# Weight chunks spread differently over the slots, and the mean of the first token group behind the scores: thresholded attention followed by a feed-forward block

## The chip, the cores and the metric

The kernel runs on one core of one Trainium2 chip. The metric is the time of one execution in device microseconds (us), the median of several runs. The engines are named as in the profile: PE (TensorE, with its weight loads as PEld), DVE (VectorE), ACT (ScalarE), POOL (GpSimd) and SP (SyncE, which here issues nearly all DMAs). Each engine works through its own instructions in the order in which the program wrote them; semaphores order the engines among each other.

## The reference

Inputs are q, k, v of 8 batches, 8 heads, 576 tokens and 64 features in float32, a scalar tau, a gain g_ln of 512, and two weights, 512 x 2048 and 2048 x 512. The weights come as float64: the kernel gets their raw 64-bit words and makes float32 of them itself.

```python
scores = scale * np.matmul(q, k.transpose(0, 1, 3, 2))
thresh = np.max(scores, axis=-1, keepdims=True) - tau
scores = np.where(scores >= thresh, scores, -1000000000.0)
scores = scores - np.max(scores, axis=-1, keepdims=True)
attn = np.exp(scores)
attn = attn / (np.sum(attn, axis=-1, keepdims=True) + 1e-09)
attn_out = np.matmul(attn, v)
# (B,H,S,D) -> x of (B, S, H*D)
mu = np.mean(x, axis=-1, keepdims=True)
var = np.mean((x - mu) ** 2, axis=-1, keepdims=True)
xn = (x - mu) / np.sqrt(var + 1e-06) * g_ln
ch = np.maximum(xn @ w_ch1, 0.0) @ w_ch2
out = x + ch
```

## The kernel before

**Slots.** The attention is cut into 72 slots, nine for each batch (`SLOTS`), handled by the loop `for n in range(NS)`. A slot takes 128 rows of each of four score blocks: two heads (h = 0 and 1, one PSUM region `sc` each) by two blocks of queries. The first four slots of a batch take the first 256 queries of a head pair, the fifth (s equal to `HP`, which is 4) takes the last 64 queries of all heads, and the last four take the second 256. In one slot these steps follow each other, and they are spread over this slot and the next two:

- `turn` (L345) transposes the q and k of the pair needed in the next slot, on DVE, after POOL has scaled q (L356). `load_qk` fetches them through SP.
- `scores` (L391, L408) writes the two `sc` regions on PE.
- `exponentials` (L414): DVE takes the negated row maxima (`neg`, L422), POOL makes the thresholds from them (`thr`, L426), ACT makes the exponentials (L436).
- `weights` (L438): DVE masks the exponentials by the threshold and sums them (L443). It reads `sc`, so the scores of the next slot cannot be written before it. In batch 0 ACT then makes diagonal matrices of the reciprocal sums (L457).
- In batch 0 `turn_weights` (L473) transposes and scales the weights on PE (`tp` and `tr`), with ACT copying out (L493, L516); later batches transpose on DVE (L533), store to a DRAM scratch (L538) and load it again (L547, L552).
- `values_of` (L565, L591, L601) multiplies with v on PE; ACT copies the result into the token group's `x` (L609, L614), and POOL adds up the features in `sum` (L643).

**Groups.** A batch holds two token groups of 288 tokens. When a group is complete, `group_ready` arranges its `mean_of` (a PE product with a matrix of 1/512, L652), `centre` (DVE subtracts the mean, L666) and `ffn_steps`, the feed-forward part as a queue of PE products (L101: `p` and `seg`). `second_part` feeds products from this queue between the attention steps, four times a slot. Group 0 is ready in slot 6 (`ready(0)` is 24 quarters). PE's order is thus fixed when the program is built.

**Weights.** The 32 weight chunks of 512 KB (16 of w1, then 16 of w2) go through the class `Weights`:

- `fetch(most)` issues up to that many loads on SP (L252), as far as there are free rooms; the rooms are places in tiles that are not needed yet.
- `begin_to(count)` begins chunks until so many have been begun: two DVE instructions (L271, L275) and two on ACT (L279, L283) each.
- `carry_all` adds the low words on POOL (L289) and frees the raw room; `mask_all` finishes a chunk on DVE (L298); `scale_all` multiplies a w1 chunk by g_ln on POOL (L310).

The table `BEGUN` gives, for each slot, the count of chunks begun by three places in the slot: after the scores' second half has been prepared, behind the masking, and at the slot's end. The feed-forward products need w1 in the order of the chunks, and then w2.

**Warm products.** `constants(times)` issues that many PE products of constants whose result is not read; there are 22 ahead of slot 0 and 8 ahead of the scores of slots 2, 3 and 4.

Of the kernel before, what the change touches and what calls it, by code (L numbers as in the profile page):

```python
# [18 lines left out]
def kernel(  # L19
# [36 lines left out]
    HP = H // 2  # L56
# [39 lines left out]
    def product(out, lhsT, rhs, **flags):  # L96


        for h in range(2):
            r = slice(64 * h, 64 * h + 64)  # L100
            nc.tensor.matmul(out[r], lhsT=lhsT[:, r], rhs=rhs, **flags)  # L101
# [239 lines left out]
    def by_blocks(u):  # L341

        return units[u][0] > 0
# [47 lines left out]
    def scores(b, s):  # L391


        hp, half = (s, 0) if s < HP else (s - HP - 1, 1)

        pieces = []
        for h in range(2):
            t = 0
            for j in range(2):
                first = FREE + j * S  # L400
                for at, n in span(first, S):
                    pieces.append((t, h, j, at, n, at - first))
                    t += n
        for t, h, j, at, n, o in sorted(pieces):
            r = slice(64 * h, 64 * h + 64)
            for i in range(2):
                qT, kT, ql = turned[b * HP + (2 * j + i if s == HP else hp)]
                nc.tensor.matmul(  # L408
                    sc[h][64 * i : 64 * i + 64, at : at + n],
                    lhsT=ql[r] if s == HP else qT[r, half, j * 128 + 64 * i : j * 128 + 64 * i + 64],  # L410
                    rhs=kT[r, o : o + n], start=True, stop=True,
                )

    def exponentials(n):  # L414


        neg = small.tile([128, 4], F32, tag="neg", name="neg")
        thr = small.tile([128, 4], F32, tag="thr", name="thr")
        es = e_room[(n + 1) % 2 if n < SLOTS else 0]
        for h in range(2):  # L420
            i = slice(2 * h, 2 * h + 2)
            nc.vector.tensor_reduce(  # L422
                out=neg[:, i], in_=pairs[h],
                axis=AXL.X, op=ALU.max, negate=True,
            )
            nc.gpsimd.tensor_scalar(  # L426
                out=thr[:, i], in0=neg[:, i], scalar1=-1.0, scalar2=low_sb,
                op0=ALU.mult, op1=ALU.add,
            )
            if h == 0:  # L430
                conversion.scale_all()
        run(n, "copy")
        for i in range(4):
            if i == 2:
                yield es, thr
            nc.scalar.activation(es[:, i], blocks[i], func=AF.Exp, bias=neg[:, i : i + 1])  # L436
# [254 lines left out]
    def run_first(calls):  # L691
        for fn in calls[:1]:
            calls.pop(0)
            fn()

    def run_all(calls):
        now = calls[:]
        calls.clear()
        for fn in now:
            fn()  # L700
# [236 lines left out]
    def ffn_steps(g):  # L937
        rb = yield from first_part(g)
        yield from (second_quarters if g else second_plain)(g, rb)
# [3 lines left out]
    QUARTERS = 4  # L943
# [10 lines left out]
    def at_quarter(n, i, fn, *args):  # L954
        later_calls.setdefault((n, i), []).append((fn, args))

    def run(n, i):
        for fn, args in later_calls.pop((n, i), ()):
            fn(*args)

    def ready(g):

        if g < 2:
            return (24, 42)[g]
        b, t = divmod(g, 2)
        return QUARTERS * (b * SLOTS + (HP, 2 * HP)[t] + 2) + (2, 4)[t]

    def second_part(n, i):

        nonlocal issued, owed, part, now  # L970
        part, now = i, QUARTERS * n + i
        if not queue:
            return
        at = QUARTERS * n + i
        g = sum(issued >= e for e in ends)
        left = sum(ROOM[t % QUARTERS] for t in range(at, ready(g + 1))) if g + 1 < NG else 0
        owed += (ends[g] - issued) * ROOM[i] / left if left > 0 else 8


        got = 1 if i in (0, QUARTERS - 1) else 2  # L980
        while queue and (owed >= 0.5 or got == 1 and i in (0, QUARTERS - 1)):
            got, cost = next(queue[0], (None, 0))
            if got is None:
                queue.pop(0)
                got = 1
            elif got == 0:
                owed = 0.0
                break
            else:
                issued += cost  # L990
                owed -= cost

    def group_ready(g):
        first = divmod(ready(g), QUARTERS)
        before = divmod(ready(g) - 1, QUARTERS)
        at_quarter(*before, mean_of, g)
        at_quarter(*(first if g and first[1] else before), centre, g)
        at_quarter(*first, lambda: queue.append(ffn_steps(g)))

    conversion = Weights()  # L1000
    if w_ch1.dtype == I64:
        conversion.fetch(4)
    else:
# [10 lines left out]
        conversion.scaled = conversion.n1  # L1014

    BEGUN = [
        (0, 0, 2), (3, 3, 4), (6, 6, 7), (9, 9, 10), (12, 12, 13), (15, 15, 16),
        (18, 20, 21), (23, 25, 26), (28, 30, 31), (32, 32, 32),
    ]

    def constants(times):

        warm = ps_ff.tile([128, QH], F32, tag="ff", name="warm")
        for _ in range(times):
            product(warm[:, :128], lhsT=avg_sb, rhs=ident, start=True, stop=True)
# [4 lines left out]
    for n in range(NS):  # L1030
        b, s = divmod(n, SLOTS)
        masks_at, behind_at, end_at = BEGUN[min(n, len(BEGUN) - 1)]
        run(n, -3)
        if 1 < n <= HP:
            constants(8)
        scores(b, s)
        run(n, -2)
        run(n, -1)
        rest = exponentials(n)
        es, thr = next(rest)  # L1040
        run(n, 0)
        if n >= HP:
            conversion.fetch(2)
        run_first(stores)
        second_part(n, 0)
        while drops and drops[0][0] is nc.gpsimd:
            drops.pop(0)[-1]()
        next(rest, None)

        u = (n + 1) // SLOTS * HP + (n + 1) % SLOTS  # L1050
        if (n + 1) % SLOTS < HP and u < len(units):
            turn(u)
            if u + 1 < len(units):
                load_qk(u + 1)
        if n < HP:
            conversion.fetch(2)
        if n < SLOTS + HP:
            run_all(aside)
        conversion.mask_all()
        conversion.begin_to(masks_at)  # L1060
        conversion.carry_all()
        conversion.scale_all()
        run(n, 1)
        second_part(n, 1)
        blocks_go = by_blocks(b * HP)
        diags = weights(es, thr, blocks_go)
        run_all(aside)
        drip()
        if n < SLOTS:
            run_all(stores)  # L1070
        conversion.mask_all()
        conversion.begin_to(behind_at)
        run(n, 2)
        second_part(n, 2)
        conversion.carry_all()
        box = []
        if blocks_go:
            scr = turn_blocks(s, es)
            at_quarter(n + 1, 0, lambda s=s, scr=scr, box=box: box.append(fetch(s, scr)))
        else:  # L1080

            made = turn_weights(s, es, diags)
            for i, at in enumerate(
                (-1, -1, 0, 0) if s <= HP else (-1, -1, -1, -1) if s < 2 * HP else (-1, 0, 1, 2)
            ):
                if i < 3:
                    at_quarter(n + 1, at, next, made)
                else:
                    at_quarter(n + 1, at, lambda made=made, box=box: box.append(next(made)))
        at_quarter(  # L1090
            n + 1, 1 if b == 0 and s <= HP else 3,
            lambda b=b, s=s, box=box: values_of(b, s, box[0]),
        )
        if s in (HP, 2 * HP):
            group_ready(2 * b + (s > HP))
        run_all(aside)
        drip({nc.vector: 4, nc.gpsimd: 6})
        conversion.fetch(2)
        if n >= HP + 2:
            conversion.mask_all()  # L1100
        run(n, 3)
        if b == 0 and s < HP - 2:
            load_v(s + 2)
        elif n >= SLOTS - 2 and (n + 2) % SLOTS < HP and n < NS - 2:
            load_v((n + 2) // SLOTS * HP + (n + 2) % SLOTS)
        second_part(n, 3)
        conversion.begin_to(end_at)
        conversion.carry_all()
        run_all(aside)
        drip({nc.vector: 2, nc.gpsimd: 0})  # L1110
# [40 lines left out]
```

## Time and profile before

| what | value |
|---|---|
| median of 3 runs | 1389.49 us (1386.02 to 1389.49) |
| profiled execution | 1386.68 us |
| its span, first to last instruction | 1384.9 us, mean granted clock 0.991 |
| busy: PE | 1329.0 us (96%), 17544 instructions |
| busy: PEld | 1002.4 us (72%) |
| busy: DVE | 922.7 us (67%) |
| busy: ACT | 455.3 us (33%) |
| busy: POOL | 617.9 us (45%) |
| DMA | 206.88 MB, mean 149 GB/s |

A busy share is an average over the whole span; the change concerns the first sixth of it, so the profile is read there, slot by slot. In the trace before, the scores of slots 0 to 6 start at 10.06, 18.42, 32.63, 46.86, 60.51, 71.80 and 88.84 us, those of slots 7 to 10 at 117.92, 141.09, 163.80 and 187.88 us. In lines of a timeline the columns are start and duration in us, engine, line, operation, what is written and read, and the count; in brackets stands the idle time before it and what ended it. In lines on waits the numbers are the sum in us, how often, and the longest. "SPq" is SP's queue issuing a DMA.

### The profile page before, as it was taken

The numbers are of one execution on the slowest core, as the hardware profiler recorded it, in microseconds if no ns is written. First come the engines' busy times: TensorE is split into PE (matmuls) and PEld (weight loads), VectorE is DVE, ScalarE is ACT, GpSimd is POOL, SyncE is SP. The second block draws the span as 40 slices with busy tenths as digits, with TensorE's granted clock in tenths as the row PEclk, the third lists the DMA queues.
The fourth block names the chain that finished last, engine by engine and source line by source line (L and its number), as shares of the span: only waits on it lengthen the run. The fifth ranks groups of instructions, "written<-read, shape, count | busy, mean of one in ns | idle before, by whom it ended". The sixth has DMA issues, their size and how long they took to land.

```text
span 1384.9 us, 40781 instructions
## 1 busy us (share of the span) xinstructions
PE 1329.0 (96%) x17544; PEld 1002.4 (72%) x17544; DVE 922.7 (67%) x1638; ACT 455.3 (33%) x991; POOL 617.9 (45%) x823
## 2 busy tenths in 40 slices
PE   6878989999999999999999999999999999999996
PEld 5755655867768696877869687776868677686966
DVE  6987867676776767657776667657776767766211
ACT  4766523232332323232232323323232323323120
POOL 3554344544443544443444455353444445344313
PEclk9999999999999999999999999999999999999998
DMA  9912255447734576447754476345763476443211
GB/s 207 267 49 70 66 145 156 160 145 184 203 131 164 139 197 178 145 143 187 200 158 147 152 198 183 135 164 154 190 187 132 144 186 186 135 160 134 58 17 18
DMA packets 322020, 206.88 MB, mean 149 GB/s; under 512 B 247984, under 2 KB 279472, under 8 KB 313776
## 3 DMA queue, kind: packets, MB, share of 16 engines
q1 hardware_dynamic: 317072, 203.68, 50.8%
q8 instruction: 138, 2.26, 0.7%
q10 hardware_dynamic: 4736, 0.59, 0.4%
q14 instruction: 42, 0.34, 0.1%
q0 software_dynamic: 32, 0.00, 0.0%
HBM read 120.46 MB, written 83.76 MB: 147 GB/s over the span
## 4 chain that ended last, share of the span: by engine, by line
PE 86%; DVE 5%; issue 2%; DMA 2%; POOL 2%; ACT 2%; SPq 1%; POOLq 0%; DVEq 0%; ACTq 0%
PE p L101 37%; PE seg L101 27%; PE sc L408 9%; PE sc L591 8%; PE sc L601 2%; DVE neg L422 1%; DMA v_rest<-in_v_dram 1%; PE tp L101 1%; DVE e L443 1%; PE mean L101 1%; PE var L101 0%; POOL sum L643 0%; POOL q_in L356 0%; SPq L136 0%; ACT e L436 0%
## 5 line engine op out<-in xcount | busy, mean ns | idle before, releaser
L101 PE MATMUL p<-xc,w 128*64 128x288 f32 x4096 | 518.1, 408 | 14.6 <-ACT hidden L795 5.0
L101 PEld LDWEIGHTS p<-xc,w 128*64 128x64 f32 x4096 | 288.2, 137 | 222.3 <-issue 15.8
L422 DVE TENSOR_REDUCE neg<-sc 128x2 f32<-128x1152 f32 x144 | 188.7, 1351 | 241.7 <-PE sc L408 241.2
L101 PE MATMUL seg<-hidden,w 128*64 128x144 f32 x3840 | 248.3, 287 | 3.8 <-DVE hidden L865 3.8
L101 PEld LDWEIGHTS seg<-hidden,w 128*64 128x64 f32 x3840 | 234.8, 137 | 15.6 <-issue 7.5
L459 POOL TENSOR_SCALAR e<-e,den 128x576 f32<-128x576 f32 x252 | 194.0, 782 | 114.9 <-DVE den L448 114.9
L443 DVE SCALAR_TENSOR_TENSOR e<-sc,thr,e 128x576 f32<-128x576 f32 x288 | 221.9, 809 | 19.8 <-POOL thr L426 14.4
L426 POOL TENSOR_SCALAR thr<-neg,low_sb 128x2 f32<-128x2 f32 x144 | 42.4, 295 | 424.3 <-DVE neg L422 422.2
L795 ACT ACTIVATE hidden<-p 128x288 f32<-128x288 f32 x256 | 106.4, 416 | 324.1 <-PE p L101 324.0
L436 ACT ACTIVATE e<-sc,neg 128x576 f32<-128x576 f32 x288 | 197.6, 754 | 4.8 <-DVE neg L422 4.8
L533 DVE STREAM_TRANSPOSE et<-e 128x1152 f32<-128x1152 f32 x112 | 153.1, 1373 | 18.3 <-POOL e L459 17.5
L408 PE MATMUL sc<-kT,qT 64*64 64x384 f32 (+3 forms) x2048 | 144.5, 413 | 11.2 <-DVE e L443 10.4
L591 PE MATMUL sc<-em,v_in 128*64 128x128 f32 (+1 forms) x2368 | 129.5, 263 | 0.0
L591 PEld LDWEIGHTS sc<-em,v_in 128*64 128x64 f32 x2368 | 122.9, 137 | 7.8
L101 PE MATMUL seg<-hidden,stage 128*64 128x144 f32 x1920 | 123.3, 286 | 0.0
L101 PEld LDWEIGHTS seg<-hidden,stage 128*64 128x64 f32 x1920 | 117.6, 137 | 2.9 <-issue 2.9
L408 PEld LDWEIGHTS sc<-kT,qT 64*64 64x64 f32 x2048 | 78.0, 136 | 56.2 <-issue 24.1
L614 ACT COPY x<-sc 128x128 f32<-128x128 f32 x120 | 31.7, 266 | 247.7 <-PE sc L408 181.2
L865 POOL TENSOR_TENSOR hidden<-hidden 128x576 f32<-128x576 f32 x60 | 84.8, 1427 | 47.5 <-ACT hidden L795 37.9
L880 ACT COPY part<-seg 128x288 f32<-128x288 f32 x75 | 30.2, 403 | 198.4 <-PE seg L101 194.3
L865 DVE TENSOR_TENSOR hidden<-hidden 128x576 f32<-128x576 f32 x60 | 49.1, 853 | 48.8 <-PE seg L101 45.8
L101 PE MATMUL seg<-hidden,e 128*64 128x144 f32 x960 | 65.3, 286 | 0.0
(149 smaller groups left out, 1131.3 us busy)
## 6 DMA issues: line engine op xcount, KB each, us to landing
scr<-et SPq DMA_DIRECT2D x63, 1152.0 KB, 5.0
em<-scr SPq DMA_DIRECT2D x63, 1024.0 KB, 5.7
out_dram<-ot SPq DMA_DIRECT2D x256, 36.0 KB, 3.8
q_in<-in_q_dram SPq DMA_DIRECT2D x124, 72.0 KB, 2.5
k_in<-in_k_dram SPq DMA_DIRECT2D x120, 72.0 KB, 2.8
er<-scr SPq DMA_DIRECT2D x126, 64.0 KB, 5.2
w<-in_moe_w_ch_dram SPq DMA_DIRECT2D x14, 512.0 KB, 5.8
v_in<-in_v_dram SPq DMA_DIRECT2D x28, 256.0 KB, 5.4
```

What stands on the lines that cost most here:

```text
L101: nc.tensor.matmul(out[r], lhsT=lhsT[:, r], rhs=rhs, **flags)
L408: nc.tensor.matmul(sc[h][64 * i : 64 * i + 64, at : at + n], lhsT=ql[r] if s == HP else qT[r, half, j * 128 + 64 * i : j * 128 + 64 * i + 64],
L422: nc.vector.tensor_reduce(out=neg[:, i], in_=pairs[h], axis=AXL.X, op=ALU.max, negate=True,)
L426: nc.gpsimd.tensor_scalar(out=thr[:, i], in0=neg[:, i], scalar1=-1.0, scalar2=low_sb, op0=ALU.mult, op1=ALU.add,)
L436: nc.scalar.activation(es[:, i], blocks[i], func=AF.Exp, bias=neg[:, i : i + 1])
L443: nc.vector.scalar_tensor_tensor(out=es[:, i], in0=blocks[i], scalar=thr[:, i : i + 1], in1=es[:, i], op0=ALU.is_ge, op1=ALU.mult, accum_o ...
L459: nc.gpsimd.tensor_scalar(out=es[:, i], in0=es[:, i], scalar1=den[:, i : i + 1], scalar2=1.0, op0=ALU.mult, op1=ALU.mult,)
L533: nc.vector.transpose(et[:, :, 64 * h : 64 * h + 64].rearrange("p n (j c) -> p j n c", j=2), es[:, 2 * h : 2 * h + 2].rearrange("p j (n c) ...
L591: nc.tensor.matmul(dst[64 * h : 64 * h + 64], lhsT=vt[:, h, c, :], rhs=pick(em[:, 2 * j : 2 * j + 2, c], h), start=c == 0 and first, stop= ...
L614: nc.scalar.copy(x_of(2 * b + (s > HP))[:, s % (HP + 1), 128 * j : 128 * j + 128], pv[j])
L795: nc.scalar.activation(hidden[:, d], p1, func=AF.Relu)
L865: eng.tensor_tensor(out=out[at], in0=in0[at], in1=in1[at], op=op)
```

## The change

1. `BEGUN`: by the end of slots 0 to 9 there were 2, 4, 7, 10, 13, 16, 21, 26, 31 and 32 chunks begun (fewer where a fetch had not yet been made); after the change there are 2, 4, 6, 8, 10, 12, 18, 24, 30 and 32.
2. In the first four slots one of the two calls `fetch(2)` goes, so two chunks are fetched a slot; from slot 4 on the two calls fetch up to three.
3. The mean of group 0 is issued one step later, behind the scores of slot 6 instead of ahead of them (the place −1 of the slot that `run(n, -1)` works off). The centring of group 0 is placed likewise.
4. 26 warm products are issued ahead of the scores of slot 1.

```diff
     def group_ready(g):
         first = divmod(ready(g), QUARTERS)
-        before = divmod(ready(g) - 1, QUARTERS)
+        before = divmod(ready(g) - 1, QUARTERS) if g else (first[0], -1)
         at_quarter(*before, mean_of, g)
         at_quarter(*(first if g and first[1] else before), centre, g)
...
     BEGUN = [
-        (0, 0, 2), (3, 3, 4), (6, 6, 7), (9, 9, 10), (12, 12, 13), (15, 15, 16),
-        (18, 20, 21), (23, 25, 26), (28, 30, 31), (32, 32, 32),
+        (0, 0, 2), (3, 3, 4), (5, 5, 6), (7, 7, 8), (9, 9, 10), (11, 11, 12),
+        (14, 16, 18), (20, 22, 24), (26, 28, 30), (32, 32, 32),
     ]
...
-        if 1 < n <= HP:
-            constants(8)
+        if 0 < n <= HP:
+            constants(8 if n > 1 else 26)
         scores(b, s)
         run(n, -2)
         run(n, -1)
...
         if n >= HP:
-            conversion.fetch(2)
+            conversion.fetch(3)
         run_first(stores)
...
         run_all(aside)
         drip({nc.vector: 4, nc.gpsimd: 6})
-        conversion.fetch(2)
+        if n >= HP:
+            conversion.fetch(3)
         if n >= HP + 2:
             conversion.mask_all()
```

## The prediction

> **What bounds the kernel now.** I read the page's slices first, then busy time by slot, then who TensorE (PE) waited for, then the timelines. The slices:
>
> ```profile
> PE   6878989999999999999999999999999999999996
> ...
> DMA  9912255447734576447754476345763476443211
> ```
>
> A slice is 34.6 us. PE is full from the fourth on; there a changed wait elsewhere is worth nothing unless PE waits too. The first three hold the idle time. By slot (columns: stretch, length, busy time of PE, weight loads, DVE, ACT, POOL, granted clock, DMA share, GB/s):
>
> ```profile
> 18.40:32.60 14.20, 13.53 (x176) 10.07 (x176) 11.74 (x24) 10.02 (x21) 5.34 (x7) 0.83 1.06 270
> 32.60:46.90 14.30, 11.46 (x180) 9.24 (x178) 12.57 (x24) 10.10 (x21) 7.01 (x10) 1.00 0.91 221
> 46.90:60.50 13.60, 12.76 (x176) 9.78 (x176) 12.81 (x26) 9.62 (x19) 6.55 (x9) 0.87 0.89 259
> 60.50:71.80 11.30, 8.82 (x147) 7.16 (x145) 11.20 (x16) 9.56 (x22) 8.98 (x9) 1.00 0.81 258
> 71.80:88.80 17.00, 10.62 (x196) 7.95 (x196) 15.12 (x27) 13.53 (x33) 13.57 (x18) 0.98 0.30 94
> ...
> 208.70:1384.90 1176.20, 1152.83 (x15348) 878.58 (x15340) 762.08 (x1356) 340.73 (x756) 520.02 (x704) 1.00 0.52 152
> ```
>
> Slots 1 to 5: DVE is busy 83% to 99% of each, the transfers take the 16 DMA engines until slot 4, and PE follows. From 208.7 us on PE is 98% busy. What PE waited for from 10 to 90 us:
>
> ```profile
> PE sc L408 <- DVE e L443: 10.4, 6, 6.2
> PE mean L101 <- POOL sum L643: 5.1, 1, 5.1
> PE tr L507 <- ACT em L493: 3.2, 4, 1.4
> ```
>
> PE waits for DVE to free the score banks, and once for the sums ahead of the mean of group 0. The place:
>
> ```profile
> 82.16 0.64 PE L601 MATMUL pv<-er,v_rest 128*64 128x64 f32 x16
> 87.91 1.00 PE L101 MATMUL mean<-sum,avg_sb 128*64 128x288 f32 x4 [5.11 <-POOL sum L643]
> 88.84 3.50 PE L408 MATMUL sc<-kT,qT 64*64 64x384 f32 x32
> 92.28 3.75 PE L101 MATMUL tp<-diag,e 128*64 128x128 f32 x64
> ```
>
> The scores of slot 6 stand behind the waiting mean, though their banks are free at 85.2 us (the last masking step on DVE).
>
> **What the Trainium skill says.** "TensorE: Matmul & The Clock Gate", section "What's actually happening": PE is throttled by default, and some 3.4 us of activity lift that. The trace agrees: after 6.19 us of idling the scores of slot 1 took 5.31 us, against 2.17 in slot 0. "SBUF — State Buffer", section "SBUF: two separate sides": a DVE operation with two SBUF inputs and a GpSimd operation lock each other out for a whole instruction. The trace agrees: the mask (L298) at 60.34 us took 1.77 us, ending 0.6 after POOL's add (60.26 to 61.55); without such a neighbour it takes 0.68. "DMA: Bandwidth & Descriptors", section "Issuing engines are not separate DMA queues": all transfers share 16 engines and interleave; so a chunk fetched early delays a key needed now. The trace fits: DMA share 0.9 to 1.06, and DVE waiting 1.59 us for k_in at 39.92.
>
> **The change part by part.** Prices of a chunk, start to start: DVE 0.45 (L271) + 0.61 (L275) + 0.60 (L298) = 1.66 us; ACT 0.57 + 0.57; POOL 1.29 (L289), and 0.68 (L310) for a w1 chunk.
>
> *26 warm products in slot 1.* 52 instructions more. 32 records of such products took 1.92 us, so 104 take 6.2, and at the rate of the first ones (6.91 us for 88) 8.2. They start at 12.2; the scores could not start before 18.42 (banks). They end at 18.4 to 20.4; the scores then take 2.1 instead of 5.3 and end by 20.6 to 22.5, before 23.7. But DVE then waits for k_in until 27.10 as before (its load stands ahead of every fetch that is removed). Value 0; bounds 1 us gained and 1 lost.
>
> *Fewer fetches and one chunk less in each of slots 2 to 5.* Slot 1 keeps its two chunks, so the scores of slot 2 stay at 32.6 (second half 33.9 to 36.0). Behind them PE runs transposes, values and the warm products until 45.03 whatever DVE does. Two chunks (1.05 MB, 3.9 us at 270 GB/s) no longer stand ahead of k_in: it lands near 36 instead of 39.92, before the reduce ends at 38.25, so that wait goes. DVE then: transposes 1.48, mask 0.57, one chunk begun instead of two 1.06, masking from 41.4 instead of 45.26, done 44.5. The scores of slot 3 now wait for PE itself: 45.0 to 47.1, where they ended at 51.6. **4.5 us.**
>
> Slot 3, on PE: transposes 3.75, wait for the copy 0.6, tr, values and rest 3.0, warm 1.9: scores of slot 4 from 56.3 to 58.4 (DVE is done masking at 54.6). Before: 60.51 to 62.6, and DVE reached the reduce only at 64.53, now at 58.3. **4.2 us on PE, 6.2 on DVE.**
>
> Slot 4, no warm products: DVE reduce 2.54, mask and begin 1.7, masking (second half behind ACT's exponentials) to 66.0; scores of slot 5 end at 67.9 instead of 75.4. **7.5 us.** Next late is the chain reduce, exponentials, masking, scores, some 9.7 us a slot.
>
> Slot 5: values end at 75.3, masking at 75.5. *The mean behind the scores:* the scores go at once and end at 77.5. ACT and POOL each have a chunk less ahead of the copies (L609) and sums (L643): copies end at 76.3, POOL's carry and scale at 77.2, three sums 1.3; mean at 78.5 (was 87.91). Behind it on PE stand the transposes, 79.4 instead of 92.28, and on DVE the centring (L666, 1.5 us) and now the slot-6 reduce: 81 to 83.5, still ahead of its exponentials, which wait for the copies of the transposed tiles at 83. First product of the feed-forward part at 84.1 instead of 96.71. **12.6 us**, of which the hidden scores are 3.4.
>
> I take off 1.6 us for lock-outs between DVE and POOL that this adds up without (one such mask, 1.1 us over, and half of another). **11.0.**
>
> *Six a slot in slots 6 to 8, two in slot 9.* Laid beside each other, PE's orders from the slot-6 transposes on are equal. Slots 6 to 9 get one chunk more each. Slot 6: its begin (1.06) fits DVE's 4.46 us of idling before 120.08, its 1.14 on ACT ends near 120.4, before the copy at 121.11; POOL's four w1 scales (2.7 us) now stand between the two thresholds of slot 7, ready near 125.6 against masking at 126.2 and the first product that needs them near 135. Slot 7: the slot-8 reduce comes 1.06 late, and 2.81 us of waiting for q_in behind it takes that up. Slot 8: 1.66 against 1.34 of idling. On SP the fetches of chunks 23 to 27 wait for rooms freed near 121 to 130 us, needed from 141. Value 0 until slot 9.
>
> *The last chunk.* Its fetch, before at 157.97 on SP, stands after the change behind the scratch store:
>
> ```profile
> 157.97 0.45 SPq L252 DMA_DIRECT2D et<-in_moe_w_ch_dram  x1
> ...
> 182.51 0.36 SPq L538 DMA_DIRECT2D scr<-et  x1
> 182.96 0.39 SPq L131 DMA_DIRECT2D v_in<-in_v_dram  x1
> ```
>
> With about 1 us of lateness it goes out near 183.9 and, beside 1.15 MB of scratch, lands near 190 (5.2 us is the median landing; 11.4 the longest). DVE has its begin (1.06) and a product of rb (0.46) queued before the slot-10 reduce: 191.5 to 192 against 190.03. Behind it stand the thresholds, the sums (after POOL's carry, 1.29), the mean of group 1 on PE, and the centring that PE waited 1.86 us for, with a mask (0.6) more ahead. PE loses 2.0; bounds 0.5 and 7. The scratch reload lands some 2 us later and has ten to spare. After slot 10 nothing changes.
>
> Sum: 1386.7 − 11.0 + 2.0 = 1377.7 us against the profiled execution (span 1384.9 and 1.8 around it). The median of the runs, 1389.5, is 2.8 above that execution, the lowest 0.7 below; I add half, 1.4: **1379**.
>
> **Rivals.** A: DVE, ACT and POOL stay tightly coupled in slots 3 to 5 (DVE was at 99% in slot 4, POOL at 80%), so only the 4.5 us of slot 2 and the hidden scores (3.4) come through: 7.9 − 2 = 5.9, some 1382. Against it: PE's own work in slots 2 and 3 was within 2 us of the period.
>
> B: the front stays paced by transfers; k_in keeps its 39.92 and the later loads wait likewise. Only the hidden scores remain: 3.4 − 2 = 1.4, some 1386.5, no change. For it: the DMA share above 0.8 to 71.8 us. Against it: DVE waited for k_in only twice, 2.8 us in all.
>
> C, slower: the chunks pushed into slots 6 to 9 make DVE's strict order the bound there. At the contended prices of slot 6 (1.02 + 1.17 + 1.77 = 3.96 us a chunk) four chunks cost 15.8, and the last chunk at 11.4 us to landing 8 more: 23.8 − 11 = 12.8 later, some 1401. It decides once slots 6 to 10 give back over 15.2 us (11.0 and the 4.2 that count). Against it: DVE idles 4.5, 1.3 and 7.2 us ahead of three of the four reduces.
>
> That the change doesn't do what it says is excluded: the orders show it.
>
> **How the numbers follow.** Forecast 0.58 (1374 to 1383), A 0.21, B 0.12, C 0.09. A measurement of this kernel tells 0.3%, 4.2 us, from no change. Faster 0.79, same 0.12, slower 0.09. The range reaches from the undiminished 12.6 with the lower run's offset and a cheap last chunk (1372) to the edge of B (1386.5).
>
> **What would show it.** Right: the first L666 some 10 to 13 us earlier; scores of slot 3 at 45 us straight behind the warm products; no wait for k_in at slot 2; 2 us more of waiting at the second mean. Wrong: reduces of slots 3 to 5 still 12 us or more apart (A, B), or new PE waits on w1 or w2 between 90 and 190 us (C).

## The result, and the profile after

| | before | after |
|---|---|---|
| median | 1388.33 us (4 runs, 1386.02 to 1389.49) | 1380.97 us (4 runs, 1378.91 to 1383.39) |
| profiled execution / its span | 1386.68 / 1384.9 us | 1383.39 / 1381.4 us |

The ratio is 0.995 (95% interval 0.9926 to 0.9973): the change makes the kernel 0.5% faster. The profiled execution of after is the slowest of its four, so the two profiles differ by only 3.5 us of span where the medians differ by 7.4. The page's slices of after:

```profile
PE   8989989999999999999999999999999999999996
...
DMA  9722455447744576437744477445764476444211
```

PE's first three slices have risen from 6, 8, 7 to 8, 9, 8. Part of the transfers has moved from the first two slices to the next four: the page's first six figures of GB/s are 207, 267, 49, 70, 66, 145 before and 181, 215, 82, 87, 95, 164 after. By slot (busy times by stretch of after, the stretches cut at the starts of the scores of slots 1, 2, 3 and 4 and then from slot 11 to the end):

```profile
18.40:33.80 15.40, 11.52 (x176) 9.20 (x176) 11.47 (x24) 9.85 (x21) 5.16 (x7) 1.00 0.84 201
33.80:47.70 13.90, 12.69 (x178) 9.95 (x178) 12.00 (x26) 8.92 (x19) 5.99 (x9) 0.88 0.70 156
47.70:58.80 11.10, 10.51 (x182) 9.05 (x180) 10.12 (x19) 9.26 (x20) 6.21 (x8) 1.00 0.87 303
...
203.80:1381.40 1177.60, 1154.51 (x15348) 878.46 (x15340) 762.03 (x1356) 340.72 (x756) 520.09 (x704) 0.99 0.51 152
```

Slot 1 is longer than before (15.4 us, 14.2 before), slot 3 much shorter (11.1, 13.6). The last stretch takes 1.4 us more with the same instructions, at a clock of 0.99. PE's waits from 10 to 90 us in after (sum, times, longest):

```profile
PE sc L408 <- DVE e L443: 5.1, 6, 2.7
...
PE mean L101 <- POOL sum L643: 0.8, 1, 0.8
```

The wait for the score banks has halved (10.4 before) and the wait ahead of the mean is 0.8 (5.1). Where the first is left, PE's timeline of after shows:

```profile
29.18 1.92 PE L101 MATMUL warm<-ident,avg_sb 128*64 128x128 f32 x32
33.80 0.86 PE L408 MATMUL sc<-kT,qT 64*64 64x384 f32 x4 [2.71 <-DVE e L443]
35.28 3.49 PE L408 MATMUL sc<-kT,qT 64*64 64x384 f32 x28 [0.61 <-DVE e L443]
...
47.67 2.20 PE L408 MATMUL sc<-kT,qT 64*64 64x384 f32 x32
...
82.97 0.71 PE L101 MATMUL mean<-sum,avg_sb 128*64 128x288 f32 x4 [0.78 <-POOL sum L643]
...
88.79 7.98 PE L101 MATMUL p<-xc,w 128*64 128x288 f32 x64 [0.25 <-ACT em L493]
```

PE idles 2.71 us ahead of the scores of slot 2, and the 28 products behind take 3.49 us at a mean granted clock of 0.61 (the same 28 take 2.16 us at 1.00 in slot 1). The scores of slot 3 follow straight behind PE's own work, as forecast, but at 47.67. The first product of the feed-forward part starts at 88.79 us, 7.9 earlier than before (96.71).

How far after is ahead of before, profile against profile: 7.9 us at the scores of slot 7, 7.8 at those of slot 10, 4.9 at the second centring (195.20 against 200.11), 4.9 at the scores of slot 12, 3.2 at those of slot 13, 3.5 at the end. So the gain of the front lasts through slots 6 to 9; 2.9 us go in slot 10 and 1.7 in slot 12.

### The profile page after: what moved, and what is told of

Read it like the earlier page. It is cut to its first block, busy times and chain, and to the rows that moved or that the text cites. A ratio compares the mean times of both kernels' runs of the same rounds, so it can differ in the third digit from the quotient of the medians.

```text
span 1381.4 us, 40994 instructions
## 1 busy us (share of the span) xinstructions
PE 1334.9 (97%) x17648; PEld 1008.5 (73%) x17648; DVE 919.6 (67%) x1638; ACT 455.1 (33%) x991; POOL 616.2 (45%) x823
## 3 DMA queue, kind: packets, MB, share of 16 engines
q8 instruction: 138, 2.26, 0.7%
## 4 chain that ended last, share of the span: by engine, by line
PE 84%; DVE 7%; ACT 2%; POOL 2%; issue 2%; DMA 2%; SPq 1%; POOLq 0%; DVEq 0%; ACTq 0%
PE p L101 35%; PE seg L101 28%; PE sc L408 9%; PE sc L591 8%; PE sc L601 2%; DVE neg L422 1%; DVE e L443 1%; PE tp L101 1%; DVE w L298 1%; ACT e L436 1%; DVE w L275 1%; PE mean L101 1%; POOL sum L643 1%; SPq L116 1%; POOL q_in L356 1%
## 5 line engine op out<-in xcount | busy, mean ns | idle before, releaser
L408 PE MATMUL sc<-kT,qT 64*64 64x384 f32 (+3 forms) x2048 | 140.8, 406 | 5.3 <-DVE e L443 5.1
```

The costliest lines, as they stand in the source:

```text
L408: nc.tensor.matmul(sc[h][64 * i : 64 * i + 64, at : at + n], lhsT=ql[r] if s == HP else qT[r, half, j * 128 + 64 * i : j * 128 + 64 * i + 64],
```

## The experiments

The theory at this point: what the front had gained too little was lost in slot 1, where the new warm products come with a later k_in; what was given back at slot 10 came from the last chunk. Against it stood two doubts: each part of the change might be worth something else by itself, and the losses are differences of one execution. Each ratio is against the kernel before, run on the same chip. Runs of one kernel spread over 1 to 8 us, a trace shows one of them; so traces and medians are read side by side.

### The changed kernel again

No edit.

> The changed kernel once more, as the yardstick for the runs beside it. My theory: the change gains about 8 us up to the first feed-forward product and gives 1.5 to 3 us back at the mean of group 1 (slot 10), so 1381 us (1379 to 1384), ratio 0.995; the profile shows the first L666 within 2 us of 83.8 us and a wait of 2 to 3 us at the second mean. Rival (the whole gain is a matter of transfers that happened to land early in one run): the first L666 would lie over 3 us away from 83.8, and the ratio would be 0.998 or more.

Measured: 1382.47 us median (1377.66 to 1383.19), ratio 0.9959 [0.9946, 0.9973]; span 1381.2. The loss in slot 1 came again (k_in awaited until 28.51 us, 28.48 in after). So did the 2.76 us of waiting ahead of the second mean. PE's clock did not fall behind that wait this time: the 36 products behind it took 4.54 us, in after 6.22. In slot 12 it fell in both. The first L666 ran at 85.09 us (83.79 in after). Time, station and wait came as expected here.

### The last chunk ahead of the scratch store

```diff
         conversion.carry_all()
+        if n == SLOTS:
+            conversion.fetch(3)
         box = []
         if blocks_go:
             scr = turn_blocks(s, es)
...
         drip({nc.vector: 4, nc.gpsimd: 6})
-        if n >= HP:
+        if n >= HP and n != SLOTS:
             conversion.fetch(3)
```

In slot 9 the fetch now stands ahead of `turn_blocks`, which issues the store (L538).

> The changed kernel, with the fetch of the last weight chunk placed ahead of the scratch store of slot 9 on SP instead of behind it; nothing else moves. My theory: the last chunk lands late and holds DVE, POOL and so the mean of group 1. Then the wait at that mean falls from 2.8 to about 1.3 us, PE's clock stays at 1.0 behind it, and the run is 1.5 to 3.5 us faster than the changed kernel: 1378 us. Rival (the extra mask and carry in DVE's and POOL's order make the slot-10 reduce and sums late, whenever the chunk lands): the wait at the mean stays at 2 us or more and the time at 1381.

Measured: 1379.74 us, ratio 0.9942 [0.9931, 0.9954]; span 1378.0. SP issues the chunk at 170.43 us instead of behind the store at 176.65 (after_again). PE's timeline of after, at the second mean:

```profile
187.53 0.71 PE L101 MATMUL mean<-sum,avg_sb 128*64 128x288 f32 x4 [2.79 <-POOL sum L643]
188.06 6.22 PE L101 MATMUL p<-hidden,w 128*64 128x288 f32 x36
195.79 4.59 PE L101 MATMUL p<-xc,w 128*64 128x288 f32 x36 [1.50 <-DVE xc L666]
```

and of this kernel:

```profile
187.24 0.71 PE L101 MATMUL mean<-sum,avg_sb 128*64 128x288 f32 x4 [1.20 <-POOL sum L643]
187.78 4.54 PE L101 MATMUL p<-hidden,w 128*64 128x288 f32 x36
193.98 4.59 PE L101 MATMUL p<-xc,w 128*64 128x288 f32 x36 [1.67 <-DVE xc L666]
```

The wait is 1.20 us again, as before the change, and the clock stays up. The chunk behind the store is what lengthened the wait. By medians the edit brings 2.7 us, though the intervals of the two ratios overlap; in the traces, from the scores of slot 10 to the centring, 1.6 us against after_again and 3.1 against after.

### Without the warm products

```diff
-        if 0 < n <= HP:
-            constants(8 if n > 1 else 26)
+        if 1 < n <= HP:
+            constants(8)
```

> The changed kernel without the 26 warm products ahead of slot 1. My theory: the warm products are worth nothing, since DVE waits for k_in behind them in either case; they only move the spell of low PE clock from slot 1 to slot 2, where PE then idles 2.7 us. So 0 to 1.5 us faster than the changed kernel, 1379.5 to 1381; scores of slot 1 take about 5 us again and those of slot 2 about 2.2 to 3. Rival (the clock of slot 1 is what the change lives on): 2 to 3 us slower than the changed kernel, 1383 to 1384.

Measured: 1382.78 us, ratio 0.9959 [0.9944, 0.9975]. The time is that of after_again, not the 1379.5 to 1381 expected, and yet it comes by another road: the front is 3.2 us *earlier* than after (scores of slot 7 at 106.83 us against 110.00, first centring at 80.61 against 83.79), and slot 10 gives it back. SP's queue of no_warm and then of after (start, duration of the four issues):

```profile
17.87 3.67 SPq L116 DMA_DIRECT2D q_in<-in_q_dram  x4
21.59 2.14 SPq L116 DMA_DIRECT2D k_in<-in_k_dram  x4
```

```profile
17.75 5.64 SPq L116 DMA_DIRECT2D q_in<-in_q_dram  x4
23.44 2.12 SPq L116 DMA_DIRECT2D k_in<-in_k_dram  x4
```

With the warm products SP sticks 2 us longer in the four q_in issues, and k_in goes out 1.85 us later; DVE gets it at 28.48 instead of 26.17. This is more than one pair of executions: with four chunks ahead of slot 0, the q_in issues take 4.73 to 5.64 us in the four profiles with the 26 products (after, after_again, early_last, warm_only), and k_in is there at 27.76 to 28.51; in the four without any (before, no_warm, mean_only, sched_only) they take 3.39 to 3.75, and k_in is there at 26.17 to 27.10. PE's timeline of no_warm at slot 10:

```profile
185.60 1.23 PE L101 MATMUL mean<-sum,avg_sb 128*64 128x288 f32 x4 [4.04 <-POOL sum L643]
186.61 6.91 PE L101 MATMUL p<-hidden,w 128*64 128x288 f32 x36
```

The chunk landed 7.8 us after its issue (6.6 in after), the mean waited 4.04, and the products behind it took 6.91 us for 4.54. From the scores of slot 10 to the centring this kernel needs 17.56 us, after 15.15, after_again 13.60.

### Two chunks fetched ahead of the first slot instead of four

```diff
     if w_ch1.dtype == I64:
-        conversion.fetch(4)
+        conversion.fetch(2)
```

> The changed kernel with two instead of four weight chunks fetched ahead of slot 0; each later fetch moves two chunks back. My theory: the keys of slot 2 (k_in, waited for until 28.5 us) stand behind these chunks on the 16 DMA engines; 1.05 MB less at some 270 GB/s is 3.9 us, so k_in lands near 25 us, the wait of 3.8 us shrinks below 1, and 2 to 3 us are gained up to the first L666: 1378 to 1379 us. Against it, chunk 2 is then wanted at about 28 us and may land later than that, which takes up to 2 us back. Rival (k_in is held by the small pieces of q, k and v themselves, not by chunks): k_in still lands after 27 us and the time is 1381 or more.

Measured: 1374.30 us (1374.13 to 1375.92), ratio 0.9908 [0.9895, 0.992]; span 1372.3. That is some 4 us better than expected. DVE of this kernel:

```profile
24.85 0.78 DVE L359 STREAM_TRANSPOSE kT<-k_in 128x576 f32<-128x576 f32 x1
```

No bracket stands behind the transpose: k_in is there before DVE comes to it. The mean runs at 78.42 us; the forecast, which took k_in as no obstacle, had it at 78.5. A second effect is in this edit: the last chunk no longer goes out behind the store (SP issues no chunk after 147.6 us), and the second mean waits 1.19 us. So its gain over after_again (8.2 us by medians) holds both losses: 5.8 us at the scores of slot 7 (105.46 against 111.30; 4.5 against the 110.00 of after), the rest behind slot 10. What the two chunks are worth by themselves is seen below, where the warm products are taken out.

### Each part alone

Only the mean of group 0 moved:

```diff
-        before = divmod(ready(g) - 1, QUARTERS)
+        before = divmod(ready(g) - 1, QUARTERS) if g else (first[0], -1)
```

> The kernel before with one part of the change: the mean of group 0 (and its centring) behind the scores of slot 6. My theory: the scores start at about 85.2 us, when DVE has freed their banks, and are done when the sums are (87.9), so the mean stays at 88 us and everything behind it comes 3.4 to 3.8 us earlier: 1383.5 us, ratio 0.9973. Rival (the scores go early, but the mean then waits for sums that POOL makes later, or DVE's reduce behind the centring becomes late): under 1.5 us gained, ratio 0.999 or more.

Measured: 1385.45 us, ratio 0.9986 [0.9975, 0.9996], 1.9 us faster, half of what was expected. PE's timeline:

```profile
86.87 3.33 PE L408 MATMUL sc<-kT,qT 64*64 64x384 f32 x28 [0.61 <-DVE e L443]
90.12 1.18 PE L101 MATMUL mean<-sum,avg_sb 128*64 128x288 f32 x4
```

The scores of slot 6 do go ahead of the mean, but behind 1.14 us of waiting for their banks they run at a low clock (3.33 us for 28, granted clock 0.63), and the mean at 90.12 waits for them, not for the sums. From the second half of the scores of slot 5 to the scores of slot 7 it is 42.92 us instead of 44.65. How far two executions can differ shows in front of it: up to slot 5 this kernel is the kernel before, and yet its scores of slot 4 start at 61.97 us instead of 60.51.

Only the table and the fetches:

```diff
-        (0, 0, 2), (3, 3, 4), (6, 6, 7), (9, 9, 10), (12, 12, 13), (15, 15, 16),
-        (18, 20, 21), (23, 25, 26), (28, 30, 31), (32, 32, 32),
+        (0, 0, 2), (3, 3, 4), (5, 5, 6), (7, 7, 8), (9, 9, 10), (11, 11, 12),
+        (14, 16, 18), (20, 22, 24), (26, 28, 30), (32, 32, 32),
...
-            conversion.fetch(2)
+            conversion.fetch(3)
...
-        conversion.fetch(2)
+        if n >= HP:
+            conversion.fetch(3)
```

> The kernel before with the chunk table and the fetches of the change, without the warm products and without the moved mean. My theory: DVE, ACT and POOL lose a chunk each in slots 2 to 5, and the scores of slot 5 start 7 us earlier than before; in slot 6 the mean waits again ahead of the scores, and slot 10 gives 1.5 to 4 us back to the late last chunk and PE's clock: 1384 to 1385.5 us, ratio 0.997 to 0.999, 2 to 3 us slower than the same with the mean moved. Rival (PE, not DVE, sets the pace of slots 2 to 5): the scores of slot 5 start less than 3 us earlier, and the ratio is 1.000 or more.

Measured: 1385.72 us, ratio 0.9981 [0.9972, 0.999], 2.6 us faster. The trace shows 7.1 us gained at the scores of slot 7, and a mean that waits again, ahead of the scores:

```profile
79.60 1.23 PE L101 MATMUL mean<-sum,avg_sb 128*64 128x288 f32 x4 [3.48 <-POOL sum L643]
80.75 4.12 PE L408 MATMUL sc<-kT,qT 64*64 64x384 f32 x32
```

No_warm is this kernel with the mean moved. Its scores of slot 7 come 4.0 us earlier, of which 0.4 was there at the scores of slot 5 (64.90 against 65.27). So the move is worth 3.6 us, about what its hidden scores were priced at (3.4), once the schedule has brought the front forward, and half of that by itself.

Only the warm products:

```diff
-        if 1 < n <= HP:
-            constants(8)
+        if 0 < n <= HP:
+            constants(8 if n > 1 else 26)
```

> The kernel before with the 26 warm products alone. My theory, new since the runs above: the products make PE use up its instructions earlier, a 16 KB instruction fetch then falls into 18 to 22 us, among the transfers of q and k, and the DMA engines stand half idle for 2 us behind it, so k_in of slot 2 comes 1 to 2 us later (28.4 instead of 27.1 us). Of the change this is a loss: 0 to 2 us slower than before, 1387 to 1389. Rival (chance in the landing times): k_in between 26 and 27.3 us, no hole in the transfers at 22 to 24 us, and the time of before to within 1 us or, if the higher clock of slot 1 counts, 1 to 3 us faster.

Measured: 1387.50 us, ratio 0.9994 [0.9986, 1.0002]: no difference that can be told. (The instruction fetch of which the expectation speaks is taken up further below.) In the trace k_in comes at 27.76 us (27.10 before) and the scores of slot 7 at 120.32 (117.92).

By their ratios the three parts bring 1.9 + 2.6 + 0.8 = 5.3 us, all together 5.7 (after_again) to 6.9 (the first comparison); within the intervals the times add up (the 0.8 of the warm products is itself no more than noise), though the traces show that the stations on the way do not.

### Are the warm products needed with k_in early?

Against two_first:

```diff
-        if 0 < n <= HP:
-            constants(8 if n > 1 else 26)
+        if 1 < n <= HP:
+            constants(8)
```

> The changed kernel with two instead of four chunks fetched ahead of slot 0, and without the 26 warm products. My theory: with k_in landed early, DVE in slot 1 waits for nothing else than PE's scores, so their 5.3 us at the low clock count now: the reduces of slot 1 end near 25.8 instead of 24.7 us, and the run is 0.5 to 1.5 us slower than the same with the products: 1375 to 1376. Rival (the products cost more through the transfers than they bring through the clock): 1 to 2 us faster, 1372.5 to 1373.5.

Measured: 1375.64 us (1375.15 to 1375.76), ratio 0.991 [0.9898, 0.9923]. By ratios the same as two_first; in the trace the scores of slot 7 come at 106.39 instead of 105.46. Where k_in does not wait, the warm products are worth 0.9 us at the front; where it does, they cost 3.2.

Beside no_warm this run also shows what the two chunks cost by themselves: without warm products, the scores of slot 7 come at 106.39 us with two chunks ahead of slot 0 and at 106.83 with four, a difference of 0.4. At the front, then, the early chunks and the warm products were dear only together. What two_first_cold gains on no_warm comes later: from the scores of slot 10 to the centring it needs 12.23 us (17.56 in no_warm), since its last chunk no longer stands behind the store, and slot 12 takes 18.05 us (19.74).

### As much warming by fewer instructions

What links idle constants on PE with a stuck SP queue? The traces show a DMA queue of the kind "instruction" with 138 packets of 16 KB. I take them for PE's instructions, as PE has 35,088 in before, ten times those of the other engines together, and as the packets come earlier when PE is given more; the trace does not name the engine. In after one falls at 20 to 22 us, in before the first behind the start at 30 to 32. So 7 products of 512 columns took the place of the 26 of 128:

```diff
+        if n == 1:
+            wide = ps_ff.tile([128, 512], F32, tag="ff", name="wide")
+            for _ in range(7):
+                product(wide, lhsT=avg_sb, rhs=turned[0][1][:, :512], start=True, stop=True)
-        if 0 < n <= HP:
-            constants(8 if n > 1 else 26)
+        if 1 < n <= HP:
+            constants(8)
```

> The changed kernel with 7 warm products of 512 columns in place of the 26 of 128 in slot 1: the same 6 us of PE, 56 PE instructions with their weight loads where there were 208. My theory: what delays k_in of slot 2 is the 16 KB instruction fetch that the many small products bring forward to 20 to 22 us; with few instructions the fetch falls later, the transfers show no hole at 22 to 24 us, k_in is there at 26 to 27.3 instead of 28.4 us, and the first L666 comes at 80.5 to 82.5 instead of 83.8 to 85.1; 1 to 3 us faster than the changed kernel, 1379 to 1381. Rival (a busy PE itself, or the earlier end of the scores, delays the transfers): the hole and 28.4 us stay, and the time too.

Measured: 1379.05 us (1378.08 to 1382.75), ratio 0.9944 [0.993, 0.9957]; k_in at 27.01 us, the first L666 at 82.62, the scores of slot 7 at 108.83 (110.00 in after, 111.30 in after_again). The interval overlaps those of after and after_again, so what follows rests on the traces. The busy times by stretch from 22 to 24 us, first of after, then of warm_wide; the last two columns are DMA share and GB/s:

```profile
22.00:24.00 2.00, 1.95 (x34) 1.70 (x32) 2.00 (x3) 2.00 (x4) 1.93 (x2) 1.00 0.39 59
```

```profile
22.00:24.00 2.00, 2.00 (x34) 1.73 (x32) 2.00 (x3) 2.00 (x5) 1.87 (x2) 1.00 0.85 125
```

The engines do the same work in both; in after the transfers have a hole, while SP is stuck at q_in. One issue is stuck there, the third of the four. SP's timeline of after and, behind it, of warm_wide:

```profile
20.96 1.81 SPq L116 DMA_DIRECT2D q_in<-in_q_dram  x1
```

```profile
25.87 1.88 SPq L136 DMA_DIRECT2D v_in<-in_v_dram  x1
```

In after the packet starts at 20.86 us, in warm_wide at 25.89, behind k_in. The third q_in issue takes 0.50 us in warm_wide and in no_warm. The same holds in all 13 profiles: an SP issue that starts within 0.5 us of the first packet behind 18 us takes 1.4 to 2.2 us. That is 1.3 of the 1.85 us by which k_in goes out late. The k_in of warm_wide, at 27.01, lies among those of the kernels without such products (26.17 to 27.10).

The front of warm_wide is still later than that of no_warm, by 2.0 us at the scores of slot 7, and k_in explains 0.8 of it. PE idles 1.15 us ahead of its scores of slot 2, and the second half runs at a granted clock of 0.62:

```profile
33.81 3.35 PE L408 MATMUL sc<-kT,qT 64*64 64x384 f32 x28 [0.61 <-DVE e L443]
```

In before, with k_in at 27.10, the same 28 start at 33.90 and take 2.16 us.

The same in two_first:

> The changed kernel with two chunks fetched ahead of slot 0 and the 7 wide warm products in slot 1. My theory: k_in is early here in any case (before 24.9 us), so DVE waits for it no more and the fetch of instructions costs nothing: within 1 us of the same with the 26 small products, 1373.5 to 1375. Rival (q and k of the next slots gain from the instruction fetch moving away too): 1 to 2 us faster, 1372 to 1373.

Measured: 1375.73 us (1374.26 to 1376.21), ratio 0.9913 [0.9899, 0.9926]; the scores of slot 7 at 105.47 us. And two_first itself again, beside it:

> The changed kernel with two instead of four chunks fetched ahead of slot 0, once more, as the yardstick beside it. My theory: 1374.3 us, ratio 0.991, within 1 us. Rival (its advantage was one lucky pair of landing times): 1377 us or more.

Measured: 1375.74 us (1374.01 to 1375.86), ratio 0.9912 [0.9899, 0.9926]; the scores of slot 7 at 105.36. This is 1.4 us above the first measurement, by the ratios the same. With k_in early the form of the warming makes no difference that can be told. The best version is two_first, with or without warm products: in both comparisons 0.991 of the time before, some 12 us, against 6 to 7 of the change.

## Why the prediction was right, and where a step was off

**Direction and range.** The measured median, 1380.97 us, is 2 us above the forecast and within its range. That it came so near is partly luck. The forecast counted on 9.0 us between the profiled executions and 10.5 between the medians; measured were 3.3 and 7.4. Three steps of the account make up the missing 5.7 us between the profiles: 3.1 at the front (7.9 for 11.0), 0.9 at the last chunk (2.9 for 2.0) and 1.7 in slot 12 (for nothing). The profiled execution of after then happened to lie 2.4 us above its median.

By the number rival A (1382) is as near, and its front of 7.9 us is the one measured; what speaks against A are the stations. It had the front gain 4.5 us in slot 2 and the rest by the hidden scores alone. In fact the reduce of slot 3 is 1.1 us ahead of before (50.20 against 51.26), that of slot 4 3.2 (61.30, 64.53) and that of slot 5 4.3 (72.15, 76.45): slots 3 and 4, where A has nothing, brought 3.2. The gaps between these reduces are 11.1 and 10.9 us (13.3 and 11.9 before), where A and B had 12 or more. No wait on w1 or w2 came up in slots 6 to 9 (rival C), and DVE does not wait for k_in in slot 2 any more. So the mechanism forecast is the one that ran: less weight work for DVE in slots 2 to 5, paid back in part at the last chunk.

Of the signs of being right, one failed. The first L666 was to come 10 to 13 us earlier and came 5.2 earlier (83.79 against 89.02). The forecast's own stations do not give these 10 to 13 either: its mean at 78.5 us is 9.4 earlier than before; the figure belongs to the first product of the feed-forward part, which came 7.9 earlier. At the second mean the wait grew by 1.6 us (2.79 against 1.20), where 2 had been named.

**Warm products: the step that failed.** It was valued 0 with bounds of 1 us each way, "DVE then waits for k_in until 27.10 as before". The release of the clock was right (the scores of slot 1 were done at 22.05 us, "20.6 to 22.5"). But two things came with it. First, k_in came at 28.48, 28.51 and 28.43 us in the three profiles of kernels with this front. Second, PE was done with slot 1 earlier, then had nothing to do and idled 2.71 us ahead of the scores of slot 2, and these ran at a low clock: the stretch of low clock had moved from slot 1, where DVE waits for k_in anyway, to slot 2, where DVE waits for PE. The Trainium skill's page "TensorE: Matmul & The Clock Gate", section "What's actually happening", puts the throttled state behind at least one idle window of some 3.4 us; here 2.71 us and, a little later, 0.61 already went with it. The reduce of slot 2, in before and then in after:

```profile
35.71 2.62 DVE L422 TENSOR_REDUCE neg<-sc 128x2 f32<-128x1152 f32 x2
```

```profile
38.42 2.62 DVE L422 TENSOR_REDUCE neg<-sc 128x2 f32<-128x1152 f32 x2 [1.32 <-PE sc L408]
```

Of these 2.7 us, 1.4 are the later k_in (DVE begins masking slot 1 at 32.19 us instead of 30.81), and 1.3 are PE's clock (the bracket). Warm_wide, with k_in as in before, has the second part alone: DVE waits 0.75 us for these scores, and the reduce starts at 36.38.

All later stations were late by 2.5 to 4.5 us against the forecast: scores of slot 3 at 47.67 (45.0), of slot 4 at 58.76 (56.3), end of the scores of slot 5 at 71.55 (67.9), mean at 82.97 (78.5). Without the warm products the scores of slot 7 come 11.1 us before those of the kernel before: the 11.0 of the forecast's front was about right for the rest of the change (one execution against another; two of the same front differed by 1.5 us at slot 4, so the agreement to 0.1 is chance). The step asked whether the earlier scores help DVE; it asked neither what PE would do behind them nor what the added instructions bring with them.

Yet the 3.2 us at the front do not show in the medians: no_warm gave them back at slot 10, where the last chunk, issued earlier, landed later after its issue and PE's clock fell. The front's shortfall and the last chunk are thus one account. Early_last, two_first and two_first_cold, whose last chunk goes out early, keep what their fronts bring. No run here has early_last's order without the warm products.

**The hidden scores, 3.4 us:** 3.6 measured where the schedule was changed too, 1.7 alone, where the scores of slot 6 had waits of 1.14 and 0.61 us ahead of them and ran at a low clock.

**Slots 6 to 9, value 0:** held. The lead is 7.92 us at the scores of slot 7 and 7.83 at those of slot 10.

**The last chunk, 2.0 us (0.5 to 7):** the place and the cause held. SP's queue of after:

```profile
175.33 0.36 SPq L538 DMA_DIRECT2D scr<-et  x1
175.78 0.39 SPq L252 DMA_DIRECT2D stage<-in_moe_w_ch_dram  x1
```

It landed 6.6 us later, at 182.4, where 6 had been taken. The price measured was 2.9 us in after: 1.6 from the mean's wait (2.79 against 1.20), 1.7 from the lower clock of the products behind it, less 0.4 of waiting for the centring. Without the drop, in after_again, the loss is 1.4 us (13.60 us from the scores of slot 10 to the centring, 12.23 before). The forecast lies between; that the wait could cost PE's clock as well was missing.

**After slot 10 nothing changes:** wrong in both profiles of the changed kernel. The order is the same, but slot 12 took 19.73 us in after and 18.04 in before. The place, in before and then in after:

```profile
233.39 6.53 PE L101 MATMUL p<-xc,w 128*64 128x288 f32 x52 [1.96 <-ACT hidden L795]
```

```profile
228.49 8.21 PE L101 MATMUL p<-xc,w 128*64 128x288 f32 x52 [1.97 <-ACT hidden L795]
```

The same wait in front, and 1.68 us more for the same products. It came in after, after_again, no_warm, sched_only and mean_only, and not in before nor in the others: in four of the five profiles with the last chunk behind the store, and in one of the eight without. Whether the late chunk makes it likelier is open. The same section of the Trainium skill says that the window over which PE's activity is judged runs freely; that would explain why equal waits differ, but no run here tests it. The 1.68 us are of the size of the spread between runs of one kernel.

**The offset of 1.4 us** between the profiled execution and the median was of the right size for before (1388.33 against 1386.68); that the profiled execution of after would lie 2.4 *above* its median could not be known.

## What to carry to other kernels

Work that fills an idle engine ahead of a wait only moves the idle spell: ask what the engine does next, and who waits for it there. Here 26 idle products took the low clock from slot 1, where it cost nothing, to slot 2, where it cost 1.3 us. At a start that transfers pace, count what each early transfer stands in front of, and count added instructions too, since they are fetched among the data. Test such parts together: two weight chunks fetched ahead of slot 0 cost 4.5 to 5.8 us at slot 7 with the warm products and 0.4 without.

A queue places a prefetch behind a store that waits for data only at the price of that wait; issue it ahead. And put a range on an idle spell of PE of 1 us or more: in these traces the lower clock behind such spells cost up to 3.4 us (5.58 us for 32 score products behind 2.26, 2.17 at full clock), and in other executions nothing.

## What the runs showed of the hardware

- **PE's clock after short waits.** Behind idle spells of 1.97 to 2.8 us the next stretch of work sometimes took 1.68 us longer and sometimes did not: 8.21 us (granted clock 0.79) against 6.53 (1.00) behind 1.97 and 1.96, 6.22 (0.73) against 4.54 (1.00) behind 2.79 (after) and 2.76 (after_again). Spells of 1.15 and then 0.61 us were followed by 3.35 us for 28 products (0.62), where 2.16 is the time at 1.00.
- **Instruction fetches beside data.** 16 KB packets of the kind "instruction" come through the DMA engines, and 26 more small products (208 instructions with their weight loads) moved one from 30 to 20 us. In all 13 profiles the first packet behind 18 us goes together with one DMA issue on SP of 1.4 to 2.2 us, where the issue that was stuck in after takes 0.50 us in no_warm and warm_wide. In stretches of 2 us, the DMA share then falls to between 0.36 and 0.57, in the packet's own stretch or the next, in 11 of the 13; in before and warm_wide it does not. That moving the packet took the hole away from k_in is shown; why a packet holds up an issue on SP is not.
